# Layer norm, attention and a gated branch on one core: hi/lo splits of later chunks moved to POOL from a plain copy, and PSUM banks released by tile

## The chip, the cores and the metric

The kernel runs on one core of a Trainium2 chip. The metric is device time in microseconds (us), the median of several runs. TensorE (PE in the profile, PEld its weight loads) multiplies into PSUM; VectorE (DVE), ScalarE (ACT) and GpSimd (POOL) work beside it; SyncE (SP) issues the DMAs of this kernel, in its own order. In this kernel POOL works on SBUF tiles only, never on PSUM.

## The reference

```
xn = layernorm(x)                                     # x: 2048 x 512, eps 1e-5
q, k, v = split(xn @ wqkv)                            # 32 heads of 16
p = softmax(q @ k.T / 4)                              # per head
s = (p @ v, heads joined) @ wo
g = silu(((xn @ w_gate) * (xn @ w_up)) @ w_down)      # w_gate, w_up: 512 x 1792
out = x + s * g
```

All of it is float32. The kernel reaches its precision on a reduced matmul type by splitting each operand into a high half (rounded) and a low half (the rest), and adding three products: high x high, high x low, low x high. So a matrix that is to be multiplied needs two halves, and making them is the work that this case is about.

## The kernel before, in words

The 2048 rows are 16 tiles of 128 (`tt`), in four chunks of 512 (`c`). The kernel has three stages.

**The prologue** is `early()` (L614 to L709). It loads the rows and weights, norms and turns chunk 0, and then issues 265 numbered steps. Each step takes the next matmul of a stream that goes through k(0), q(0), v of tiles 0 to 2, k(1), q(1), v 3, k(2), v 4 and 5, k(3), v 6 to 15 (L694): k(c) and q(c) are the projections of chunk c for the first group of heads, 12 matmuls each. A table (`at`, L678 to L693) hangs other work on steps: the statistics of a tile (`ln_stats`, L170), the root (`ln_root`, `ve`, L178), the scale (`ln_scale`, L181, a chain of six small VectorE operations, L184 to L189, the first a reciprocal), the normalization (`ln_apply`, on ScalarE but for one tile), and the turning (`ln_turn`, L198). Turning transposes a tile with four matmuls into one PSUM bank; then ScalarE reads the bank and writes the high half `xh` (L204), and VectorE reads the bank again and writes the low half `xl` (L211). A projection ends likewise: ScalarE writes the high half `hl[:, 0]` (`qk_high`, L277), VectorE the low half from the same bank (`qk_out`, L281), and SP stores both to DRAM and reloads them in the layout that the scores want (`qk_store`, `load_k`, `load_q`).

The list `EARLY` (L39) puts groups of four score matmuls on the steps 57, 66, 75, 84 (keys of chunk 0), 98, 108, 118, 128 (chunk 1), 138 and on (chunk 2), 178 and on (chunk 3). A score bank is free when VectorE has reduced it to its maxima (`mx`, L549).

The prologue's PSUM pool (`EARLY_BUFS`, L40) has four banks for scores and the first four turned tiles ("s"), two for the other turned tiles and q(0) ("x"), and two for projections ("f"). Then `banks_of` (L88) opens another pool (`BUFS`, L41) on the same eight banks: two for the transposed scores "st", three "s", one "pv", two "misc".

**The middle** (L778 to L808) has 512 rounds: four transposed-score matmuls (`t`, L572), their exponentials on ScalarE (L574), four score matmuls of a later group (`s`, L547), the sums over values (`pv`, L583), and some matmuls of a filler: the other projections (`proj_pair`, where POOL already makes the halves from an SBUF copy `qr`, L271 and L272), and the gated branch.

**The tail** is the last filler (`ending`, L424): the output projection in pairs of tiles into the two "misc" banks (`z`, L238 and L242), and for each tile `end` (L408): a product with the gate, a sum with x, and a store. In the last 21 rounds and behind them VectorE does both (L411, L412): the product goes back into the PSUM bank, and the sum reads it there. Up to then VectorE does the product (L414) and POOL the sum (L415).

Within PE, ACT and DVE the order of instructions is the order in which the program writes them (`manual_schedule` with `ORDERED`, L44). For SP and POOL a scheduler chooses the order when the program is built. In all cases an engine works its instructions off in its order, so a waiting one holds those behind it.

Of the kernel before, what the change touches and what calls it, by code (L numbers as in the profile page):

```python
# [11 lines left out]
F32 = mybir.dt.float32  # L12
# [34 lines left out]
def body(ctx, tc, x, wqkv, wo, wg, wu, wd, out):  # L47
# [4 lines left out]
    def dma(dst, src):  # L52
        nc.sync.dma_start(dst, src)
# [33 lines left out]

    def banks_of(bufs):  # L88
        stack = ExitStack()
        fst["ps"] = stack.enter_context(tc.tile_pool(name="ps" + "".join(bufs), bufs=1, space=PSUM)), bufs  # L90
        return stack

    def psum(tag, name):
# [47 lines left out]
        nc.gpsimd.tensor_tensor(lo, raw, hi, op=OP.subtract)  # L141
        return hi, lo

    def split_rows(src, raw, wh, wl, queue, early):
        for d in range(len(raw)):
            queue.dma_start(raw[d], src[d * P:(d + 1) * P])
            if early:
                nc.scalar.activation(wh[d], raw[d], AF.Copy)
            else:
                nc.gpsimd.tensor_copy(wh[d], raw[d])  # L150
            nc.gpsimd.tensor_tensor(wl[d], raw[d], wh[d], op=OP.subtract)
        return wh, wl

    norm = {}

    def tokens(tt):
# [38 lines left out]
            return nc.vector.tensor_scalar(xt, xt, e[:, t:t + 1], mr[:, t:t + 1], op0=OP.mult, op1=OP.add)  # L195
        return nc.scalar.activation(xt, xt, AF.Identity, bias=mr[:, t:t + 1], scale=e[:, t:t + 1])

    def ln_turn(tt, low=True):  # L198
        c, t = divmod(tt, 4)
        xt = tokens(tt)  # L200
        norm["x", tt] = pt = psum("x" if c else "s", f"xT{tt}")
        for d in range(ND):
            nc.tensor.transpose(pt[:, d * P:(d + 1) * P], xt[:, d * P:(d + 1) * P], ident)
        nc.scalar.activation(xh[c][:, :, t * P:(t + 1) * P], pt.rearrange("p (d q) -> p d q", d=ND), AF.Copy)  # L204
        if low:
            ln_low(tt)

    def ln_low(tt):
        c, t = divmod(tt, 4)
        sl = slice(t * P, (t + 1) * P)  # L210
        nc.vector.tensor_tensor(xl[c][:, :, sl], norm["x", tt].rearrange("p (d q) -> p d q", d=ND), xh[c][:, :, sl],  # L211
                                op=OP.subtract)
# [40 lines left out]
    def qk_proj(w, m, which, c, tag):  # L253
        wh, wl = w
        o = psum(tag, f"p{which}_{m}_{c}")
        hi, lo = [lambda d, w=w: w[:, d] for w in (wh, wl)]
        yield from full(o, ((hi, lambda d: xh[c][:, d]), (lo, lambda d: xh[c][:, d]), (hi, lambda d: xl[c][:, d])))
        qk_out(o, qk_high(o), m, which, c)

    def proj_pair(m, which):  # L260

        outs = []
        yield from pair(outs, [("misc", f"p{w}_{m}_{c}") for _, w, c in which],
                        [terms(lambda d: ws[0][:, d], lambda d: ws[1][:, d],
                               lambda d: xh[c][:, d], lambda d: xl[c][:, d], ND) for ws, _, c in which])
        raws = [qp.tile([P, D], F32, name="qr", bufs=2) for _ in outs]
        fst["high"] = nc.scalar.activation(raws[0], outs[0], AF.Copy)
        nc.vector.tensor_copy(raws[1], outs[1])
        for o, (_, w, c) in zip(raws, which):
            hl = qp.tile([P, 2, D], F32R, name="hl", bufs=HBUFS)  # L270
            nc.gpsimd.tensor_copy(hl[:, 0], o)  # L271
            nc.gpsimd.tensor_tensor(hl[:, 1], o, hl[:, 0], op=OP.subtract)  # L272
            qk_store(hl, m, w, c)

    def qk_high(o):
        hl = qp.tile([P, 2, D], F32R, name="hl", bufs=HBUFS)
        nc.scalar.activation(hl[:, 0], o, AF.Copy)  # L277
        return hl

    def qk_out(o, hl, m, which, c):  # L280
        nc.vector.tensor_tensor(hl[:, 1], o, hl[:, 0], op=OP.subtract)  # L281
        qk_store(hl, m, which, c)

    def qk_store(hl, m, which, c):

# [36 lines left out]
    def ffn(nxt):  # L322
        fp = fst["fp"]
        for c in range(NC):
# [7 lines left out]
            for ti, fs in enumerate(THIRDS):  # L332
# [20 lines left out]
                if c == NC - 1 and fs[-1] == NF - 1:  # L353
                    fst["y"] = y
                    fst["w"] = [keep.tile([P, ND, D], F32R, name=n) for n in ("fh", "fl")]
                    for d in range(ND):
                        raw = fp.tile([P, D], F32, name="wdr", bufs=2)
                        split_rows(wo[d * P:(d + 1) * P], [raw], *[[t[:, d]] for t in fst["w"]], nc.sync, False)
                for t in range(0, 4, 2):
                    outs = []  # L360
                    yield from pair(outs, [("misc", f"y{c}_{ti}_{u}") for u in (t, t + 1)], [terms(lambda i: hh[:, i, u * P:(u + 1) * P],
# [45 lines left out]

    def end(c, t, o, yt, xt):  # L408
        tt = 4 * c + t
        if now[0] >= NU * 16 - LEAD and c < NC - 1 or t % 2 and c == NC - 1:  # L410
            nc.vector.tensor_tensor(o, o, yt, op=OP.mult)  # L411
            nc.vector.tensor_tensor(yt, o, xt, op=OP.add)  # L412
        else:
            nc.vector.tensor_tensor(yt, o, yt, op=OP.mult)  # L414
            nc.gpsimd.tensor_tensor(yt, yt, xt, op=OP.add)  # L415
        dma(out[tt * P:(tt + 1) * P], yt)

    def o_terms(c, t):
# [195 lines left out]
    def early():  # L614
# [17 lines left out]
        def warm(n):  # L632
            for _ in range(n):
                nc.tensor.matmul(psum("x", "warm"), ident, on.rearrange("p b e -> p (b e)"), start=True, stop=True)
# [11 lines left out]
            ln_apply(tt)  # L646
        ln_stats(3)
        ln_root(first[1])
        ln_turn(0, False)
        ln_turn(1, False)  # L650
        warm(1)
        ln_scale(first[1])
        last = ln_apply(2)
        ln_apply(3)
# [1 line left out]
        ln_low(1)  # L656
        ln_turn(2)
        ln_turn(3)
        warm(1)
        wk, wq = [split_raw(f"w{which}", raw, last) for which, raw in zip((1, 0), wraw)]  # L660
        wv = [[etile().bitcast(F32R) for _ in range(ND)] for _ in range(2)]
        for d in range(ND):
# [172 lines left out]
```

## Time and profile before

| what | value |
|---|---|
| median of 3 runs | 1809.49 us (1808.87 to 1809.57) |
| the profiled execution's own time | 1810.38 us |
| its span | 1808.6 us |
| PE busy | 1791.0 us, 99% |
| DVE busy | 1480.3 us, 82% |
| ACT busy | 1237.7 us, 68% |
| POOL busy | 548.3 us, 30% |
| granted TensorE clock, mean | 0.999 of full |

The span is the time between the first and last instruction of the profiled execution; its own time has 1.8 us around that. PE's matmuls overlap, so a row with several matmuls that is longer than the same row elsewhere holds a wait that isn't shown as idle. Where a row says `[1.29 <-DVE xl L211]`, the engine stood idle for 1.29 us before it, until that instruction let it go.

### The profile page before, as it was taken

How to read it: one execution, taken by the hardware profiler on the slowest of the kernel's cores; microseconds unless marked ns; L12 is line 12 of the kernel's file. 1: busy time of each engine (PE TensorE's matmuls, PEld its weight loads, DVE VectorE, ACT ScalarE, POOL GpSimd, SP SyncE). 2: the span in 40 equal slices, each digit the busy share in tenths (PEclk: the TensorE clock that was granted, in tenths of full speed). 3: DMA queues.
4: the chain of work that ended last, by engine and by line, in shares of the span. 5: the costliest groups of instructions: out<-in, count | busy, mean ns of one | idle time of the engine just before them, and what ended most of it. 6: DMA issues, size and time to landing. Idle time of an engine off the chain costs nothing.

```text
span 1808.6 us, 34173 instructions
## 1 busy us (share of the span) xinstructions
PE 1791.0 (99%) x13572; PEld 991.8 (55%) x13572; DVE 1480.3 (82%) x2472; ACT 1237.7 (68%) x2365; POOL 548.3 (30%) x615
## 2 busy tenths in 40 slices
PE   8999999999999999999999999999999999999998
PEld 5655555555555555555555555555555555555555
DVE  7878888888888888888888888888888888888832
ACT  5257676777776767777677777776767767767664
POOL 2012322531322234233132441431325323224340
PEclk9999999999999999999999999999999999999999
DMA  5515422611231132311124220511125111111342
GB/s 199 142 63 201 177 106 112 161 46 33 63 74 49 37 99 75 74 51 51 28 65 110 68 63 24 103 51 40 43 80 120 48 44 51 40 42 51 116 154 71
DMA packets 117228, 145.73 MB, mean 81 GB/s; under 512 B 12620, under 2 KB 74060, under 8 KB 114380
## 3 DMA queue, kind: packets, MB, share of 16 engines
q1 hardware_dynamic: 117068, 143.55, 27.8%
q8 instruction: 106, 1.74, 0.4%
q14 instruction: 54, 0.44, 0.1%
HBM read 95.94 MB, written 47.45 MB: 79 GB/s over the span
## 4 chain that ended last, share of the span: by engine, by line
PE 95%; DVE 2%; DMA 1%; ACT 1%; issue 0%; POOL 0%; SPq 0%; DVEq 0%; ACTq 0%
PE pv L583 28%; PE t L572 21%; PE s L547 12%; PE y L238 6%; PE u L238 5%; PE g L238 5%; PE u L242 4%; PE g L242 4%; PE p L238 3%; PE y L242 2%; PE v L219 2%; PE z L238 1%; PE z L242 1%; PE p L242 1%; DMA ks<-KD 0%
## 5 line engine op out<-in xcount | busy, mean ns | idle before, releaser
L549 DVE TENSOR_REDUCE mx<-s 128x1 f32<-128x512 f32 x2048 | 1312.0, 684 | 246.1 <-PE s L547 156.0
L574 ACT ACTIVATE e<-t 128x512 f32<-128x512 f32 x2048 | 1111.7, 596 | 430.5 <-PE s L547 267.3
L572 PE MATMUL t<-qs,ks 50*128 50x512 f32 x2048 | 705.1, 426 | 1.6 <-ACT V L299 0.8
L547 PE MATMUL s<-ks,qs 48*128 48x512 f32 x2048 | 699.9, 427 | 0.8 <-DMA ks<-KD 0.6
L572 PEld LDWEIGHTS t<-qs,ks 50*128 50x128 f32 x2048 | 347.2, 185 | 500.8 <-ACT e L574 473.1
L583 PE MATMUL pv<-e,V 128*32 128x512 f32 x4096 | 545.7, 605 | 0.0
L547 PEld LDWEIGHTS s<-ks,qs 48*128 48x128 f32 x2048 | 337.6, 184 | 23.5 <-DVE mx L549 7.3
L583 PEld LDWEIGHTS pv<-e,V 128*32 128x32 f32 x4096 | 81.0, 108 | 156.4 <-issue 147.2
L138 POOL CAST w0h<-w0r 128x512 fp32r<-128x512 f32 x60 | 36.7, 611 | 414.9 <-PE u L238 216.0
L351 POOL CAST dh<-wdr 128x512 fp32r<-128x512 f32 x56 | 33.6, 611 | 184.0 <-PE y L242 103.1
L242 PE MATMUL u<-fh,w0h 64*128 64x512 f32 x224 | 88.2, 394 | 0.4 <-DVE h L347 0.4
L242 PE MATMUL y<-dh,hh 64*128 64x512 f32 x224 | 88.2, 394 | 0.0
L238 PE MATMUL u<-fh,w0l 64*128 64x512 f32 x224 | 87.8, 392 | 0.0
L238 PE MATMUL g<-fh,w1l 64*128 64x512 f32 x224 | 87.8, 392 | 0.0
L238 PE MATMUL u<-fh,w0h 64*128 64x512 f32 x224 | 87.6, 391 | 0.0
L238 PE MATMUL g<-fl,w1h 64*128 64x512 f32 x224 | 87.6, 391 | 0.0
L238 PE MATMUL y<-dh,hl 64*128 64x512 f32 x224 | 87.6, 391 | 0.0
L242 PE MATMUL g<-fl,w1h 64*128 64x512 f32 x224 | 87.6, 391 | 0.0
L238 PE MATMUL u<-fl,w0h 64*128 64x512 f32 x224 | 87.6, 391 | 0.0
L238 PE MATMUL y<-dh,hh 64*128 64x512 f32 x224 | 87.5, 391 | 0.0
L238 PE MATMUL g<-fh,w1h 64*128 64x512 f32 x224 | 87.5, 391 | 0.0
L238 PE MATMUL y<-dl,hh 64*128 64x512 f32 x224 | 87.5, 391 | 0.0
(249 smaller groups left out, 2853.0 us busy)
## 6 DMA issues: line engine op xcount, KB each, us to landing
w1r<-in_wg_dram SPq DMA_DIRECT2D x56, 256.0 KB
w0r<-in_wu_dram SPq DMA_DIRECT2D x56, 256.0 KB
wdr<-in_wd_dram SPq DMA_DIRECT2D x56, 256.0 KB
qs<-QD SPq DMA_DIRECT2D x64, 192.0 KB
ks<-KD SPq DMA_DIRECT2D x12, 768.0 KB
KD<-hl SPq DMA_DIRECT2D x16, 512.0 KB
QD<-hl SPq DMA_DIRECT2D x16, 512.0 KB
OD<-tr SPq DMA_DIRECT2D x31, 256.0 KB
```

The lines of the kernel that those rows point to most:

```text
L138: cast = nc.gpsimd.tensor_copy(hi, raw)
L219: nc.tensor.matmul(o, l(d), r(d), start=k == d == 0, stop=k == 2 and d == ND - 1)
L238: nc.tensor.matmul(outs[k], l[LOWER], r[LOWER], start=k == 0 and n == 0, stop=(stop or k == 0) and n == len(low) - 1, skip_group_check=k == 1)
L242: nc.tensor.matmul(outs[1 - k], l[UPPER], r[UPPER], start=k == 0 and m == 0, stop=(stop or k == 0) and m == len(high) - 1, skip_group_chec ...
L351: nc.gpsimd.tensor_copy(dh[:, i], raw)
L547: nc.tensor.matmul(o, QS[i][b:b + KB, pr, t * P:(t + 1) * P], k[b:b + KB, pr, kc * 512:(kc + 1) * 512], start=True, stop=True)
L549: nc.vector.tensor_reduce(MX[i][:, j, t, kc:kc + 1], o, axis=AX.X, op=OP.max)
L572: nc.tensor.matmul(o, k[b:b + KR, pr, kt * P:(kt + 1) * P], QS[i][b:b + KR, pr], start=True, stop=True)
L574: nc.scalar.activation(e, o, AF.Exp, scale=DH ** -0.5)
L583: nc.tensor.matmul(fst["pv"][32 * j:32 * j + 32], V[:, kt, h0:h0 + 32], es[j], start=kt == 0, stop=kt == NT - 1)
```

## The change

For chunks 1 to 3, `ln_turn` and `qk_proj` call a new function `halves`: ScalarE makes a plain float32 copy of the PSUM bank into an SBUF tile `qr`, and POOL makes the high half and the low half from that copy. `qr` has three buffers instead of two. Chunk 0 keeps ScalarE and VectorE. The two single `warm` matmuls between the first turned tiles go. `banks_of` opens its pools with `reuse_waits="tile"`: a tile that lies on a bank of a closed pool waits for the tiles that lay on that bank, and not for the whole pool. In `end`, a late tile writes the product to SBUF, where the sum then reads it. `proj_pair` and the split of `wo` call the new `split_rows` and issue what they issued before.

```diff
@@ -87,7 +87,7 @@
 
     def banks_of(bufs):
         stack = ExitStack()
-        fst["ps"] = stack.enter_context(tc.tile_pool(name="ps" + "".join(bufs), bufs=1, space=PSUM)), bufs
+        fst["ps"] = stack.enter_context(tc.tile_pool(name="ps" + "".join(bufs), bufs=1, space=PSUM, reuse_waits="tile")), bufs
         return stack
 
     def psum(tag, name):
@@ -140,16 +140,6 @@
             tc.add_manual_dep(cast.ins, after.ins.name, BEHIND, reason="keeps the port free for the layer norm")
         nc.gpsimd.tensor_tensor(lo, raw, hi, op=OP.subtract)
         return hi, lo
-
-    def split_rows(src, raw, wh, wl, queue, early):
-        for d in range(len(raw)):
-            queue.dma_start(raw[d], src[d * P:(d + 1) * P])
-            if early:
-                nc.scalar.activation(wh[d], raw[d], AF.Copy)
-            else:
-                nc.gpsimd.tensor_copy(wh[d], raw[d])
-            nc.gpsimd.tensor_tensor(wl[d], raw[d], wh[d], op=OP.subtract)
-        return wh, wl
 
     norm = {}
 
@@ -195,15 +185,30 @@
             return nc.vector.tensor_scalar(xt, xt, e[:, t:t + 1], mr[:, t:t + 1], op0=OP.mult, op1=OP.add)
         return nc.scalar.activation(xt, xt, AF.Identity, bias=mr[:, t:t + 1], scale=e[:, t:t + 1])
 
-    def ln_turn(tt, low=True):
+    def halves(o, hi, lo):
+
+        raw = qp.tile([P, D], F32, name="qr", bufs=3)
+        first = nc.scalar.activation(raw, o, AF.Copy)
+        split_rows(raw, hi, lo)
+        return first
+
+    def split_rows(raw, hi, lo):
+        if len(hi.shape) == 3:
+            raw = raw.rearrange("p (d q) -> p d q", d=ND)
+        nc.gpsimd.tensor_copy(hi, raw)
+        nc.gpsimd.tensor_tensor(lo, raw, hi, op=OP.subtract)
+
+    def ln_turn(tt):
         c, t = divmod(tt, 4)
         xt = tokens(tt)
         norm["x", tt] = pt = psum("x" if c else "s", f"xT{tt}")
         for d in range(ND):
             nc.tensor.transpose(pt[:, d * P:(d + 1) * P], xt[:, d * P:(d + 1) * P], ident)
-        nc.scalar.activation(xh[c][:, :, t * P:(t + 1) * P], pt.rearrange("p (d q) -> p d q", d=ND), AF.Copy)
-        if low:
-            ln_low(tt)
+        hi, lo = [x[c][:, :, t * P:(t + 1) * P] for x in (xh, xl)]
+        if c:
+            halves(pt, hi, lo)
+        else:
+            nc.scalar.activation(hi, pt.rearrange("p (d q) -> p d q", d=ND), AF.Copy)
 
     def ln_low(tt):
         c, t = divmod(tt, 4)
@@ -255,7 +260,13 @@
         o = psum(tag, f"p{which}_{m}_{c}")
         hi, lo = [lambda d, w=w: w[:, d] for w in (wh, wl)]
         yield from full(o, ((hi, lambda d: xh[c][:, d]), (lo, lambda d: xh[c][:, d]), (hi, lambda d: xl[c][:, d])))
-        qk_out(o, qk_high(o), m, which, c)
+        hl = qp.tile([P, 2, D], F32R, name="hl", bufs=HBUFS)
+        if c:
+            halves(o, hl[:, 0], hl[:, 1])
+        else:
+            nc.scalar.activation(hl[:, 0], o, AF.Copy)
+            nc.vector.tensor_tensor(hl[:, 1], o, hl[:, 0], op=OP.subtract)
+        qk_store(hl, m, which, c)
 
     def proj_pair(m, which):
 
@@ -263,23 +274,13 @@
         yield from pair(outs, [("misc", f"p{w}_{m}_{c}") for _, w, c in which],
                         [terms(lambda d: ws[0][:, d], lambda d: ws[1][:, d],
                                lambda d: xh[c][:, d], lambda d: xl[c][:, d], ND) for ws, _, c in which])
-        raws = [qp.tile([P, D], F32, name="qr", bufs=2) for _ in outs]
+        raws = [qp.tile([P, D], F32, name="qr", bufs=3) for _ in outs]
         fst["high"] = nc.scalar.activation(raws[0], outs[0], AF.Copy)
         nc.vector.tensor_copy(raws[1], outs[1])
         for o, (_, w, c) in zip(raws, which):
             hl = qp.tile([P, 2, D], F32R, name="hl", bufs=HBUFS)
-            nc.gpsimd.tensor_copy(hl[:, 0], o)
-            nc.gpsimd.tensor_tensor(hl[:, 1], o, hl[:, 0], op=OP.subtract)
+            split_rows(o, hl[:, 0], hl[:, 1])
             qk_store(hl, m, w, c)
-
-    def qk_high(o):
-        hl = qp.tile([P, 2, D], F32R, name="hl", bufs=HBUFS)
-        nc.scalar.activation(hl[:, 0], o, AF.Copy)
-        return hl
-
-    def qk_out(o, hl, m, which, c):
-        nc.vector.tensor_tensor(hl[:, 1], o, hl[:, 0], op=OP.subtract)
-        qk_store(hl, m, which, c)
 
     def qk_store(hl, m, which, c):
 
@@ -355,7 +356,8 @@
                     fst["w"] = [keep.tile([P, ND, D], F32R, name=n) for n in ("fh", "fl")]
                     for d in range(ND):
                         raw = fp.tile([P, D], F32, name="wdr", bufs=2)
-                        split_rows(wo[d * P:(d + 1) * P], [raw], *[[t[:, d]] for t in fst["w"]], nc.sync, False)
+                        dma(raw, wo[d * P:(d + 1) * P])
+                        split_rows(raw, *[t[:, d] for t in fst["w"]])
                 for t in range(0, 4, 2):
                     outs = []
                     yield from pair(outs, [("misc", f"y{c}_{ti}_{u}") for u in (t, t + 1)], [terms(lambda i: hh[:, i, u * P:(u + 1) * P],
@@ -407,12 +409,13 @@
 
     def end(c, t, o, yt, xt):
         tt = 4 * c + t
-        if now[0] >= NU * 16 - LEAD and c < NC - 1 or t % 2 and c == NC - 1:
+        if t % 2 and c == NC - 1:
             nc.vector.tensor_tensor(o, o, yt, op=OP.mult)
             nc.vector.tensor_tensor(yt, o, xt, op=OP.add)
         else:
+            late = now[0] >= NU * 16 - LEAD and c < NC - 1
             nc.vector.tensor_tensor(yt, o, yt, op=OP.mult)
-            nc.gpsimd.tensor_tensor(yt, yt, xt, op=OP.add)
+            (nc.vector if late else nc.gpsimd).tensor_tensor(yt, yt, xt, op=OP.add)
         dma(out[tt * P:(tt + 1) * P], yt)
 
     def o_terms(c, t):
@@ -646,9 +649,8 @@
             ln_apply(tt)
         ln_stats(3)
         ln_root(first[1])
-        ln_turn(0, False)
-        ln_turn(1, False)
-        warm(1)
+        ln_turn(0)
+        ln_turn(1)
         ln_scale(first[1])
         last = ln_apply(2)
         ln_apply(3)
@@ -656,7 +658,8 @@
         ln_low(1)
         ln_turn(2)
         ln_turn(3)
-        warm(1)
+        ln_low(2)
+        ln_low(3)
         wk, wq = [split_raw(f"w{which}", raw, last) for which, raw in zip((1, 0), wraw)]
         wv = [[etile().bitcast(F32R) for _ in range(ND)] for _ in range(2)]
         for d in range(ND):
```

## Rows read from the trace of the kernel before

**Rows 1.** The page, part 4: the chain that ended last, by engine.

```profile
PE 95%; DVE 2%; DMA 1%; ACT 1%; issue 0%; POOL 0%; SPq 0%; DVEq 0%; ACTq 0%
```

**Rows 2.** Waits; PE's timeline; a window (last three: PEclk, DMA share, GB/s).

```profile
PE xT L203 <- DVE xl L211: 2.4, 3, 1.3
...
13.77 1.17 PE L219 MATMUL p<-fh,w1h 128*128 128x512 f32 x4
...
33.77 1.90 PE L547 MATMUL s<-ks,qs 48*128 48x512 f32 x4
...
43.61 0.66 PE L203 MATMUL xT<-ident,V 128*128 128x128 f32 x4 [1.29 <-DVE xl L211]
...
48.61 0.73 PE L219 MATMUL p<-xh,w1h 128*128 128x512 f32 x2 [0.69 <-ACT V L299]
...
50.53 0.71 PE L547 MATMUL s<-ks,qs 48*128 48x512 f32 x3 [0.32 <-DMA ks<-KD]
...
12.00:14.00 2.00, 2.00 (x11) 1.23 (x11) 1.82 (x4) 1.52 (x4) 2.00 (x3) 1.00 1.05 396
```

**Rows 3.** Timeline of ACT, 10 to 66 us.

```profile
12.54 1.08 ACT L204 ACTIVATE fh<-xT 128x512 fp32r<-128x512 f32 x2 [0.48 <-PE xT L203]
...
24.71 0.58 ACT L204 ACTIVATE xh<-xT 128x512 fp32r<-128x512 f32 x1
...
55.18 0.59 ACT L277 ACTIVATE hl<-p 128x512 fp32r<-128x512 f32 x1
```

**Rows 4.** Timeline of DVE, 10 to 66 us.

```profile
18.15 1.17 DVE L178 TENSOR_SCALAR ve<-mv 128x4 f32<-128x4 f32 x1
...
19.81 0.76 DVE L185 TENSOR_TENSOR e<-r 128x4 f32<-128x4 f32 x1
...
24.28 0.67 DVE L173 BATCH_NORM_STATS2 st<-V 128x6 f32<-128x512 f32 x1
...
27.37 0.16 DVE L189 SCALAR_TENSOR_TENSOR mr<-mv,e 128x4 f32<-128x4 f32 x1
...
32.64 2.48 DVE L549 TENSOR_REDUCE mx<-s 128x1 f32<-128x512 f32 x4
```

**Rows 5.** POOL's timeline; then groups by line and form (busy, mean ns, idle before).

```profile
15.49 5.06 POOL L664 TENSOR_TENSOR e<-e 128x512 fp32r<-128x512 f32 x4
...
L272 POOL TENSOR_TENSOR hl<-qr,hl 128x512 fp32r<-128x512 f32 x26 | 33.0, 1289 | 0.0
...
L271 POOL CAST hl<-qr 128x512 fp32r<-128x512 f32 x26 | 15.2, 612 | 73.6 <-ACT qr L267 73.6
...
L211 DVE TENSOR_TENSOR xl<-xT,xh 128x512 fp32r<-128x512 f32 x12 | 8.1, 682 | 4.7 <-ACT xh L204 4.7
```

**Rows 6.** Timeline of SP, the DMA issues, 0 to 130 us.

```profile
39.22 0.83 SPq L56 DMA_DIRECT2D KD<-hl  x2
45.41 0.32 SPq L56 DMA_DIRECT2D QD<-hl  x1
...
46.41 0.93 SPq L56 DMA_DIRECT2D ks<-KD  x2
```

**Rows 7.** Timelines of PE and ACT, 64 to 126 us.

```profile
65.78 0.70 PE L547 MATMUL s<-ks,qs 48*128 48x512 f32 x3 [0.30 <-DMA ks<-KD]
...
106.96 0.46 PE L572 MATMUL t<-qs,ks 50*128 50x512 f32 x1 [0.79 <-ACT V L299]
...
106.27 0.60 ACT L299 ACTIVATE V<-v 128x512 f32<-128x512 f32 x1 [3.05 <-PE v L219]
```

**Rows 8.** Groups by line and form; one line's instructions (ns); POOL's timeline.

```profile
L242 PE MATMUL z<-fh,hl 64*128 64x512 f32 x32 | 12.8, 401 | 2.4 <-DVE hh L412 1.7 <-DVE dl L412 0.8
...
L412 DVE TENSOR_TENSOR dl<-z,dl 128x512 f32<-128x512 f32 x6 | 4.1, 692 | 0.2
...
L505 DVE TENSOR_TENSOR h<-tr,g x1: 693/693/693, 1796.8 to 1796.8; 128x512 fp32r<-128x512 f32 x1
...
1738.88 1.27 POOL L313 TENSOR_TENSOR y<-e,y 128x512 f32<-128x512 f32 x1
```

## The prediction, made before the change was run

> **What bounds the kernel now.** I read the page first: TensorE holds 95% of the chain that ended last [rows 1]. The middle, rounds of scores, exponentials and filler matmuls, has TensorE work back to back, and the change leaves its instructions alone; what moves lies in the prologue (0 to 107 us), at its end, and in the closing pairs of the output projection (from about 1724 us). There I read the timeline of TensorE for its gaps, and then the timelines of the engines named as releasers. Work on PE is in order, so a wait that goes there moves everything behind it, unless the next thing is late instead.
>
> In the prologue PE waits three times, 2.4 us in all, for the VectorE subtraction `xl` that still reads the PSUM bank which the next transposition wants; the longest is 1.29 us at 43.61 [rows 2]. A hidden one is the score group at step 66: four matmuls spread over 1.90 us from 33.77, since VectorE is late with the maxima of the group before [rows 2, 4]. Then 0.69 us at 48.61 before k(2), shown as a wait for a `V` copy; but its bank is that of q(1), which VectorE (L281) lets go at the same moment. Then 0.32 us at 50.53 for the keys of chunk 1 [rows 2] and 0.30 us at 65.78 for those of chunk 2 [rows 7].
>
> **The change, part by part. (a) Turned tiles.** For chunks 1 to 3 ScalarE makes a plain copy and POOL the two halves. ScalarE's instruction stays one PSUM read of about 0.6 us [rows 3]; VectorE loses 12 subtractions of about 0.68 us and four more in the projections; POOL gains 16 pairs, a cast of 0.61 and a subtraction of 1.29 us [rows 5], 1.9 us each, 30 us in all. POOL had nothing to do there from 20.55 us on [rows 5]. A bank is now free after ScalarE (25.29 for tile 4 [rows 3]), about 0.7 us sooner, so the three waits of 2.4 us go.
>
> What is late next: VectorE's layer-norm chain. At 18.15 `ve` took 1.17 us and at 19.81 the first multiply 0.76 us, where such operations otherwise take about 0.16 [rows 4]. Four POOL subtractions ran end to end from 15.49 to 20.55 [rows 5], 1.26 us apart, so the third ended near 19.3; the two held operations ended at 19.32 and 20.57. So a small VectorE operation of this kind waits for the end of the running POOL instruction; the reciprocal and the statistics between them were not held. The changed kernel puts POOL to work on tiles 4 to 7 from 25.3 to 32.8, right where chunk 2's chain runs. Its `ve` still comes ahead, at 25.1, behind the last statistics of 24.28 [rows 4]. Then L185 to L189, five operations, each reach the port while POOL is busy: ends at about 26.0, 27.2, 27.8, 28.4 to 29.0, and 29.7, against 27.53 before [rows 4]. Behind it on VectorE stand four statistics (0.67 us and a short second step each [rows 4], 3.3 us in all), without the two subtractions that used to lie among them; then the maxima of step 57 start at 33.05 against 32.64 [rows 4]. The step-66 scores need those banks, so PE leaves them 0.3 us **later** than before: the first two bank waits (1.1 us) are not collected. Bounds: 1.4 us gained here if nothing is held, 1.0 us lost if the maxima slip by one POOL subtraction more. I take the loss of 0.3, since the two held rows are this very chain.
>
> The Trainium skill ("GPSIMD Engine Reference", Performance versus the Vector engine) has the Vector engine about 2 times faster on elementwise work, which speaks against moving it. The rows agree on the price, 1.29 against about 0.69 us; by that rule alone the prologue would lose, but here the moved work has an idle engine, and what counts is only when each result is needed.
>
> From there: 1.29 us at 43.61 goes (chunk 3's chain, at 35.5 to 36.7, lies in a POOL gap, and the copy of tile 9 ends near 41.3, ahead of PE at 42.7). **(b) Projections.** q(1)'s bank is free after ScalarE's copy, by my reckoning near 44.4, so 0.69 us goes; k(2) could start at 46.95. It needs POOL's cast of tile 11. POOL's queue there is k(1), tiles 8 to 11, then q(1), 1.9 us each from 38.3: tile 11's cast ends by 46.7, q(1) at 49.9. It just fits.
>
> The keys of chunk 1: k(1)'s halves end at 40.2 (before, VectorE gave them at 39.2 and SP issued at once [rows 6]). A store and its reload need about 7 us (keys of chunk 2: halves done 59.0, used at 65.78 [rows 7]); 47.1 us is ahead of the need at 48.3, so the 0.32 us goes too. For chunk 2 POOL is still behind: q(1) to 49.9, tiles 12 to 14, then k(2), copied by ScalarE near 53.3 (55.18 before [rows 3]); its halves end at 57.4, the scores can start 6.8 us later, 64.2, and PE is there at 63.8: a wait of 0.4 more. Against 65.78 [rows 7] that is 1.6 us gained: +0.3 - 1.29 - 0.69 - 0.32 + 0.4. Chunk 3's keys have 0.9 us to spare.
>
> **(c) Two warm matmuls** leave PE's queue. The second pair ends where the first projection starts, 13.77, and that needs ScalarE's cast of tile 3, done at 13.62 [rows 2, 3]: 0 to 0.1 us gained. Moving `ln_low(2)` and `ln_low(3)` behind the transpositions leaves VectorE's order as it is: nothing.
>
> **(d) Banks by tile.** PE stands 0.79 us at 106.96 until the last `V` copy (106.27 to 106.87) is done, though the score-transposed matmul it wants to start writes another bank [rows 7]. Released by tile, that one can start at about 106.2; the pair of projections behind it probably takes the banks of that copy and of the last maxima, so it comes at about 106.95 instead of 107.49. I take 0.5, with 0 and 0.79 as ends.
>
> **(e) The end of late tiles.** The product now leaves PSUM at once, and the sum has both operands in SBUF; it is not faster (0.693 us for such an operation, 0.692 for the old form [rows 8]), but the second bank of a pair is free before its sum, not after. PE waits there 2.4 us, 1.7 in two places and 0.8 in a third [rows 8]. Freed 0.69 us earlier each, unless POOL holds the first sum: at 1777 POOL is idle (0.69), at 1738 its short operation ends just before (0.55; the subtraction of 1.27 us starts behind it [rows 8]), at 1724 it is in a run (0.36). Sum 1.6. Ends: 2.1 with no hold; with a hold through a whole subtraction at two places, 0.8 us lost at each, so a loss of 0.9. The final tiles on the chain of the last transposition have as many operations as before: nothing.
>
> For the sum in (e), the Trainium skill ("Advanced Engine Details and Errata", VectorE Performance Modes; the GPSIMD page adds the case of two SBUF inputs) has POOL and such VectorE instructions block each other. The two held rows of the layer norm agree; by that rule each sum waits, without it the 2.1 stands.
>
> **Sum.** 1.6 + 0.05 + 0.5 + 1.6 = 3.75 us. The profiled execution took 1810.38 us around a span of 1808.6, 0.89 above the median of 1809.49; so 1806.6 for it, and 1805.7 for the median.
>
> **The rivals.** *Keys behind the queries (slower).* SP is one queue. In the kernel before it issued the keys' load (46.41) only behind the first query store (45.41), though the key store had gone at 39.22 [rows 6]. If that order stays, the load waits for POOL's cast of q(1), the last in its queue, at 48.6, so it goes at 49.7, 3.3 us later, and the scores come 3.3 us after 50.53. With 0.5 and 1.6 regained, that is 1.2 us slower: 1810.7. It decides where the cast of q(1) comes later than about 43 us and the order is kept. Against it: the store has 8 us until then, not 6, so an order by readiness puts the load first. 10%.
>
> *Nothing is held.* If VectorE's chain slips between POOL's instructions, step 66 gains 1.4 instead of losing 0.3; some is lost again to the keys of chunk 2. 1.4 us more: 1804.3. Against it stand the two held rows. 13%.
>
> *The edges give nothing.* The sums in the tail are held and the banks at the prologue's end still wait: only 1.6 of the prologue remains, 1807.9. 12%.
>
> *The clock falls.* Without the warm pairs TensorE idles a little more before 13.77. The granted clock stood at full there [rows 2]; at the lower level (1.2 GHz) the twelve k(0) matmuls, in fours of 1.17 us at most [rows 2], about 2.8 us in all, would take twice that: about 1808.5. The transpositions lie between, so 5%.
>
> **The numbers.** The forecast holds 60%, with its own range 1804.7 to 1807.2. About 0.2% (3.6 us) is what a measurement of this kernel can tell from no change, and 1805.9 is that line: a little over half of the forecast and nearly all of the second rival lie below it. More than 0.2% slower takes the first rival with a held tail (1813), or a cost that I don't see: 9%. The range 1803.8 to 1809.7 takes in all but the first rival and small tails.
>
> **What would show it.** Right: no gap of PE behind `xl`, L185 to L189 of chunk 2 stretched to 4 us, the maxima of step 57 near 33, scores of chunk 2 near 64, first exponential near 106.9, and gaps before the z pairs down to about 0.1 to 0.4 us. Wrong: a gap of PE over 2 us for `ks<-KD`, the chain at 1.5 us beside a busy POOL, or sums in the tail over 1 us.

## The result, and the profile after

The changed kernel takes 1817.24 us (median of 6 runs, 1816.54 to 1819.25), the kernel before, run beside it, 1809.53 (1808.87 to 1810.88): 7.7 us slower, ratio 1.0044 (95% interval 1.0031 to 1.0057). The forecast was 1805.7, with 1803.8 to 1809.7 as its range. The span of the profiled execution grew from 1808.6 to 1815.7 us.

The page's part 4, the chain that ended last, by engine (it answers to [rows 1]), and of part 2 the granted clock in 40 slices:

```profile
PE 94%; DVE 2%; DMA 2%; POOL 1%; issue 0%; ACT 0%; SPq 0%; POOLq 0%; ACTq 0%; DVEq 0%
...
PEclk9899999999999999999999999999999999999999
```

The share of DMA went from 1 to 2%, and the second slice, 45 to 91 us, has a clock under 9 tenths. So the loss lies in the prologue. There TensorE's waits, from 10 to 125 us (engine, line, releaser; total, times, longest), read:

```profile
PE s L550 <- DMA ks<-KD: 8.8, 4, 7.0
...
PE p L224 <- ACT fh L211: 0.8, 1, 0.8
```

The three waits for `xl` of [rows 2], 2.4 us, are gone as the change means them to. In their place stand 8.8 us for the keys, which took 0.6 us before. (The second line is the stretch ahead of k(0) where a warming matmul used to run; k(0) starts no later for it.) TensorE's timeline shows where; these rows answer to [rows 2, 7]:

```profile
13.18 1.17 PE L224 MATMUL p<-fh,w1h 128*128 128x512 f32 x4 [0.83 <-ACT fh L211]
...
33.20 2.29 PE L550 MATMUL s<-ks,qs 48*128 48x512 f32 x4 [0.32 <-DVE mx L552]
...
46.23 0.74 PE L224 MATMUL p<-xh,w1h 128*128 128x512 f32 x2
...
54.39 0.76 PE L550 MATMUL s<-ks,qs 48*128 48x512 f32 x1 [6.98 <-DMA ks<-KD]
55.42 1.19 PE L550 MATMUL s<-ks,qs 48*128 48x512 f32 x3 [0.26 <-DMA ks<-KD]
...
61.82 0.42 PE L206 MATMUL xT<-ident,V 128*128 128x128 f32 x2
...
73.69 0.46 PE L550 MATMUL s<-ks,qs 48*128 48x512 f32 x1 [1.24 <-DMA ks<-KD]
74.47 0.70 PE L550 MATMUL s<-ks,qs 48*128 48x512 f32 x3 [0.32 <-DMA ks<-KD]
...
116.34 0.50 PE L575 MATMUL t<-qs,ks 50*128 50x512 f32 x1
```

Up to 46.23, where k(2) starts, TensorE is 2.38 us ahead of the 48.61 of [rows 2] (0.59 of it because the first rows were ready sooner: k(0) starts at 13.18 against 13.77). Then, within one step, it is 4.9 us behind: the scores of step 98 stand at 55.42 against 50.53 [rows 2]. Why the keys are late is in SyncE's timeline (issue time and duration), which answers to [rows 6]:

```profile
39.88 0.83 SPq L56 DMA_DIRECT2D KD<-hl  x2
49.21 0.80 SPq L56 DMA_DIRECT2D QD<-hl  x2
50.11 1.41 SPq L56 DMA_DIRECT2D ks<-KD  x2
```

The keys were stored at 39.88. Their load has its place in the queue behind **both** stores of q(1), where in [rows 6] it stood behind one. One of the two carries the low half of q(1), and POOL gives that last, as its timeline shows:

```profile
45.55 0.62 POOL L198 CAST xh<-qr 128x512 fp32r<-128x512 f32 x1
46.11 0.63 POOL L198 CAST hl<-qr 128x512 fp32r<-128x512 f32 x1
46.68 1.28 POOL L199 TENSOR_TENSOR xl<-qr,xh 128x512 fp32r<-128x512 f32 x1
47.91 1.28 POOL L199 TENSOR_TENSOR hl<-qr,hl 128x512 fp32r<-128x512 f32 x1
```

The subtraction ends at 49.19 and the first of the two stores goes at 49.21. The load also took longer to land. From its issue to the last three scores it is 5.3 us (50.11 to 55.42), where it was 4.1 before (46.41 to 50.53 [rows 2, 6]). The likely reason is that the store of both halves (512 KB, the other 256) now goes ahead of it and not behind: the windows below show the 16 DMA engines 0.99 and 0.95 busy while it moved. No run separates this. So of the 4.9 us by which step 98 is late, 3.7 are the later issue (50.11 against 46.41) and 1.2 the landing.

A second price hangs on the first. Windows of 2 us (busy time of PE, PEld, DVE, ACT and POOL; then PEclk, DMA share, GB/s):

```profile
50.00:52.00 2.00, 0.00 (x0) 0.00 (x0) 0.00 (x0) 0.00 (x0) 1.08 (x1) 0.91 0.99 367
52.00:54.00 2.00, 0.00 (x0) 0.00 (x0) 0.00 (x0) 0.00 (x0) 0.00 (x0) 0.50 0.95 224
...
56.00:58.00 2.00, 2.00 (x7) 1.07 (x5) 1.78 (x3) 0.00 (x0) 0.00 (x0) 0.50 0.09 9
...
62.00:64.00 2.00, 2.00 (x14) 1.28 (x13) 1.07 (x2) 1.09 (x2) 0.85 (x3) 1.00 0.03 8
```

In the wait the granted clock fell to the lower level (0.50 is 1.2 of 2.4 GHz), and it stayed there to nearly 62 us: 7 matmul records in a full window where later there are 14. From the last scores of step 98 to the turn of tile 14 TensorE needed 6.40 us (55.42 to 61.82). The kernel before needed 3.52: its turn of tile 14 came at 54.05. That is 2.9 us more.

At the keys of chunk 2 there is a wait again, 1.24 and 0.32 us, and behind it the clock reads 0.50 from 76 to 78. From 116 us on the distance hardly changes: 9.4 us at the first transposed scores (116.34 against 106.96 [rows 7]), 9.2 at the first product of the late tiles (near 1733), and 7.1 at the end, since the new end of late tiles gives 2 us back.

### The profile page after: what moved, and what is told of

It reads as the page before. It is cut to its first block, busy times and chain, and to the rows that moved or that the text cites. A ratio compares the mean times of both kernels' runs of the same rounds, so it can differ in the third digit from the quotient of the medians.

```text
span 1815.7 us, 34194 instructions
## 1 busy us (share of the span) xinstructions
PE 1794.1 (99%) x13568; PEld 991.1 (55%) x13568; DVE 1474.4 (81%) x2456; ACT 1238.3 (68%) x2365; POOL 580.7 (32%) x647
## 4 chain that ended last, share of the span: by engine, by line
PE 94%; DVE 2%; DMA 2%; POOL 1%; issue 0%; ACT 0%; SPq 0%; POOLq 0%; ACTq 0%; DVEq 0%
PE pv L586 27%; PE t L575 21%; PE s L550 11%; PE y L243 6%; PE u L243 5%; PE g L243 4%; PE u L247 4%; PE g L247 4%; PE y L247 3%; PE p L243 3%; PE v L224 2%; PE p L247 2%; PE z L243 1%; PE z L247 1%; DMA wdr<-in_wd_dram 1%; PE p L224 0%
## 5 line engine op out<-in xcount | busy, mean ns | idle before, releaser
L247 PE MATMUL g<-fh,w1h 64*128 64x512 f32 x224 | 87.7, 392 | 0.0
L243 PE MATMUL g<-fh,w1h 64*128 64x512 f32 x224 | 87.7, 391 | 0.0
```

What stands on the lines that cost most here:

```text
L243: nc.tensor.matmul(outs[k], l[LOWER], r[LOWER], start=k == 0 and n == 0, stop=(stop or k == 0) and n == len(low) - 1, skip_group_check=k == 1)
L247: nc.tensor.matmul(outs[1 - k], l[UPPER], r[UPPER], start=k == 0 and m == 0, stop=(stop or k == 0) and m == len(high) - 1, skip_group_chec ...
```

## The experiments

All runs are the median of this kernel against the kernel before on the same chip in the same rounds; the befores lay between 1809.33 and 1810.11.

**Keys first.** The changed kernel; a dependency puts the two stores of q(1) behind the load of chunk 1's keys in SyncE's queue.

```diff
...
-        dmar(dst[:, both], hl)
-        dmar(dst[:, one], hl[:, 0])
+        puts = dmar(dst[:, both], hl), dmar(dst[:, one], hl[:, 0])
+        if m == 0 and which == 0 and c == 1:
+            for put in puts:
+                tc.add_manual_dep(put.ins, fst["keys"].ins.name, ORDER, reason="keys of chunk 1 go first")
...
```

> The changed kernel, with one edge of order more on SP: q(1)'s two stores stand behind the load of chunk 1's keys. Theory A (the order on SP, and the clock that falls in the wait, are the whole loss): the keys' load is issued near 43 us, step 98 waits under 0.5 us, the granted clock stays at full from 44 to 84 us, and the time is 1804 to 1807. Rival B (POOL delivers the halves of k(1) too late, whatever the order): most of the 7 us wait stays, over 1812. Rival C (another edit, such as the warm matmuls or the held layer norm, costs the rest): the wait goes, but the time stays over 1809.5.

Measured: 1806.38 us (1803.43 to 1808.5), ratio 0.9980 (0.9972 to 0.9989). SyncE's timeline, and what waits are left on TensorE's:

```profile
40.84 0.83 SPq L57 DMA_DIRECT2D KD<-hl  x2
...
44.21 0.80 SPq L57 DMA_DIRECT2D ks<-KD  x2
...
50.20 0.81 SPq L57 DMA_DIRECT2D QD<-hl  x2
```

```profile
64.25 0.47 PE L553 MATMUL s<-ks,qs 48*128 48x512 f32 x1 [1.44 <-DMA ks<-KD]
65.09 0.70 PE L553 MATMUL s<-ks,qs 48*128 48x512 f32 x3 [0.38 <-DMA ks<-KD]
```

With nothing but the order mended the change is 3.25 us faster than before instead of 7.71 slower; the order is worth 11 us. The load went 3.4 us after its store, and step 98 no longer waits. Two things that theory A expected did not come: keys of chunk 2 are still late by 1.8 us, and behind that wait the clock reads 0.50 from 68 to 70 us.

**The split alone.** The changed kernel with the old `end` and the old release of banks; the splits on POOL stay, the warming matmuls stay out.

```diff
...
-        if t % 2 and c == NC - 1:
+        if now[0] >= NU * 16 - LEAD and c < NC - 1 or t % 2 and c == NC - 1:
...
-            (nc.vector if late else nc.gpsimd).tensor_tensor(yt, yt, xt, op=OP.add)
+            nc.gpsimd.tensor_tensor(yt, yt, xt, op=OP.add)
```

> The changed kernel with the old end of tiles and the old release of PSUM pools; the splits on POOL and the missing warm matmuls stay. Theory A: SP's order is the changed kernel's, so the wait of about 7 us and the low clock stay, and the gains at the prologue's end and in the tail (0.6 and 2.0 us by the two traces) are gone: 1819 to 1820.5. Rival C (a part of the loss comes from the new end or the new release): under 1817.

Measured: 1818.15 us (5 runs), ratio 1.0046 (1.0034 to 1.0059), with a wait of 6.50 us at step 98. That is 0.9 us under the range of the theory and 1.2 above the rival's line; all of the loss is in this part. **The end alone** and **the banks alone**, each on the kernel before:

```diff
-        if now[0] >= NU * 16 - LEAD and c < NC - 1 or t % 2 and c == NC - 1:
+        if t % 2 and c == NC - 1:
...
+            late = now[0] >= NU * 16 - LEAD and c < NC - 1
...
-            nc.gpsimd.tensor_tensor(yt, yt, xt, op=OP.add)
+            (nc.vector if late else nc.gpsimd).tensor_tensor(yt, yt, xt, op=OP.add)
```

> The kernel before with the new end of late tiles alone. Theory A: the three waits before z shrink from 2.4 to about 0.7 us, as in the changed kernel, 1807 to 1808. Rival (sums held by POOL give it back): 1809.3 to 1810.

> The kernel before with PSUM banks released by tile alone. Theory A: the 0.79 us gap at the prologue's end goes in part, 1808.7 to 1809.1. Rival (the pair behind it waits for the same banks): 1809.4 to 1809.6.

Measured: the end 1807.71 us, ratio 0.9988 (0.9979 to 0.9997), 1.9 us faster; the banks 1808.91, ratio 0.9995 (0.9986 to 1.0004), 0.7 us, which the interval does not tell from nothing. In the trace of the banks' run the 0.79 us before the first transposed scores [rows 7] is gone (this run's k(0) began at 12.83, 0.94 sooner than in [rows 2], so not all of the 2 us between 104.91 and 106.96 is the banks'):

```profile
104.91 0.50 PE L572 MATMUL t<-qs,ks 50*128 50x512 f32 x1
```

**The wait filled.** The changed kernel with eight matmuls of a constant tile in the wait.

```diff
         at[190].append((ones_rows, ks[0]))
+        at[98].append((warm, 8))
```

> The changed kernel with eight matmuls of the constant tile put into step 98, ahead of the scores that wait for the keys of chunk 1. Their results are read by nobody. The wait itself (6.98 us in the changed kernel) stays: the load of the keys still goes behind both stores of q(1). Only what TensorE does in it is different. Theory (the wait costs twice, once by itself and once by the lower granted clock behind it): the granted clock stays near 1.00 from 52 to 62 us, steps 98 to 101 take about 3.5 us as before and not 6.4, and the time falls by about 2.9 us from 1817.2 to about 1814.3, or to about 1812.8 if the second dip at 76 to 78 us, which came after a wait of 1.8 us, goes as well. Rival (the low clock is not bound to the idle stretch but to what TensorE runs then): the clock falls as before and the time stays at 1817 or goes above it.

Measured: 1812.55 us (11 runs, 1811.43 to 1813.76), ratio 1.0013 (1.0004 to 1.0021). TensorE's timeline, and two windows:

```profile
48.49 7.21 PE L637 MATMUL warm<-on,ident 128*128 128x512 f32 x16
55.63 1.24 PE L550 MATMUL s<-ks,qs 48*128 48x512 f32 x4
```

```profile
52.00:54.00 2.00, 2.00 (x6) 0.94 (x5) 0.00 (x0) 0.00 (x0) 0.00 (x0) 1.00 1.05 307
...
56.00:58.00 2.00, 1.95 (x12) 1.33 (x11) 1.84 (x4) 0.00 (x0) 0.00 (x0) 1.00 0.49 86
```

The keys come as late as in the changed kernel, but the clock stays at full behind them. Against its own before the kernel is 2.4 us slower instead of 7.7: **5.3 of the 11 us hang on TensorE standing idle in that wait**, and the rest, from 2.4 slower to the 3.25 gained with the order mended, 5.7 us, is the wait itself. The two traces show where the 5.3 us lie. The first dip is 2.9 of them. At chunk 2 the wait is 0.8 us shorter (0.37 and 0.36 instead of 1.24 and 0.32), and the dip behind it is gone: from its last three scores to the next group takes 3.1 us (71.44 to 74.58), where the changed kernel took 4.7 (74.47 to 79.18). So some 4.5 us are the lower clock. The rival falls.

**The order alone.** The kernel before, its splits untouched; only the load is put behind both stores.

```diff
...
+                    if g == 0 and cs == [1]:
+                        for put in fst["puts"]:
+                            tc.add_manual_dep(load.ins, put.ins.name, ORDER, reason="queries of chunk 1 go first")
...
```

> The kernel before, with its splits where they were, where only the load of the keys of chunk 1 is put behind both stores of q(1) in SyncE's queue (it stood behind one of them). Theory (it is the order in the queue that makes the loss, and the POOL splits make it long): the low half of q(1) is ready on VectorE about 2 us earlier than on POOL, so the load goes at about 47 to 48.5 us instead of 46.41, the scores of step 98 wait 0.5 to 2.5 us and the clock may dip; 1810 to 1814 us. Rival (the order does not matter while VectorE splits q(1)): the load still lands ahead of TensorE's need and the time stays within 0.2% of before, 1808 to 1811 us.

Measured: 1815.87 us (6 runs, 1815.51 to 1817.62), ratio 1.0032 (1.0020 to 1.0043), more than either theory gave. SyncE's timeline and TensorE's:

```profile
47.84 0.33 SPq L57 DMA_DIRECT2D QD<-hl  x1
48.28 1.19 SPq L57 DMA_DIRECT2D ks<-KD  x2
```

```profile
52.35 0.76 PE L550 MATMUL s<-ks,qs 48*128 48x512 f32 x1 [3.37 <-DMA ks<-KD]
53.39 1.19 PE L550 MATMUL s<-ks,qs 48*128 48x512 f32 x3 [0.28 <-DMA ks<-KD]
```

The load goes 1.9 us later than the 46.41 of [rows 6], or 2.7 counted from k(0), which began 0.8 sooner here (12.97). It lands late as well, 5.1 us from its issue to the last three scores (48.28 to 53.39), as in the changed kernel. That brings waits of 3.4 and 0.3 us, a clock of 0.50 from 52 to 56, and 5.8 us in all. So the order loses time even where VectorE makes the split.

**The queries split the old way**, with the keys first; and the same **with the two warming matmuls** put back.

```diff
...
-        if c:
+        if c and which:
             halves(o, hl[:, 0], hl[:, 1])
...
```

> The changed kernel with the keys of chunk 1 loaded ahead of the stores of q(1), and with the projection q(1) split the old way, high half by ScalarE and low half by VectorE; the keys' projections and the turned tiles stay with POOL. Theory (what is left of the waits, 1.4 and 0.4 us at the keys of chunk 2, comes from q(1)'s two POOL instructions standing ahead of the tiles and of k(2) in POOL's queue): these waits go or fall under 0.5 us, and the time falls by 1 to 2.5 us from 1806.4 to 1804 to 1805.4. Rival (POOL catches up between the chunks, and the wait at chunk 2 comes from the order of SyncE's queue): the waits stay and the time stays at 1806.4 give or take 0.7.

> The kernel of the run before this one with the two warming matmuls of the prologue, which the change took out, put back in their places. Theory (they cost what they last where TensorE was the last to be ready, and the clock does not need them): 0 to 1 us slower than without them. Rival (they keep the granted clock up in the first 16 us or at 36 to 40 us, where dips showed in single profiles): as fast or up to 1 us faster, with fewer slices under 1.00 in the first 70 us.

Measured: 1806.62 us (ratio 0.9981, 0.9972 to 0.9989), and 1806.09 with the warming matmuls (ratio 0.9982, 0.9973 to 0.9991). My theory of the wait at chunk 2 missed: it stayed, 1.6 and 1.9 us. The warming matmuls cost nothing that these runs can tell. POOL's timeline of the second run shows what delays the keys instead:

```profile
51.90 0.62 POOL L199 CAST hl<-qr 128x512 fp32r<-128x512 f32 x1
52.48 1.30 POOL L200 TENSOR_TENSOR xl<-qr,xh 128x512 fp32r<-128x512 f32 x1
53.73 1.28 POOL L200 TENSOR_TENSOR hl<-qr,hl 128x512 fp32r<-128x512 f32 x1
```

Between the two halves of k(2) stands a tile's subtraction, 1.3 us, and the half itself takes twice VectorE's time. So the next runs took the keys off POOL as well.

**Only the tiles on POOL.** The changed kernel, with all projections split as before; no order set by hand.

```diff
-        if c:
-            halves(o, hl[:, 0], hl[:, 1])
-        else:
-            nc.scalar.activation(hl[:, 0], o, AF.Copy)
-            nc.vector.tensor_tensor(hl[:, 1], o, hl[:, 0], op=OP.subtract)
+        nc.scalar.activation(hl[:, 0], o, AF.Copy)
+        nc.vector.tensor_tensor(hl[:, 1], o, hl[:, 0], op=OP.subtract)
```

> The changed kernel with the turned tiles of chunks 1 to 3 split by POOL, as the change has it, but with every projection of later chunks (k(1), q(1), k(2), k(3)) split as before, high half by ScalarE and low half by VectorE; no order is set by hand. In SyncE's queue the load of the keys of chunk 1 then stands behind one of the two stores of q(1), as in the kernel before. Theory (the loss comes from the projections' part of the change alone, by the place that the load gets): no wait over 1 us for keys at step 98, and 1803.5 to 1806.5 us, with the gain of the end, the banks and most of the prologue. Rival (the tiles' part makes POOL or VectorE late too, so that VectorE holds the low half of q(1) back): the load goes after 49 us and the time stays above 1811.

Measured: 1804.59 us (6 runs, 1803.9 to 1805.73), ratio 0.9971 (0.9960 to 0.9983). SyncE's timeline has the old order again, and TensorE's has waits of 0.6 us at most for keys:

```profile
42.62 0.32 SPq L56 DMA_DIRECT2D QD<-hl  x1
...
43.62 0.93 SPq L56 DMA_DIRECT2D ks<-KD  x2
44.97 0.34 SPq L56 DMA_DIRECT2D QD<-hl  x1
```

```profile
46.87 0.49 PE L547 MATMUL s<-ks,qs 48*128 48x512 f32 x1 [0.64 <-DMA ks<-KD]
...
62.76 0.69 PE L547 MATMUL s<-ks,qs 48*128 48x512 f32 x3 [0.47 <-DMA ks<-KD]
```

Which engines split the four projections k(1), q(1), k(2) and k(3) is the whole difference to the changed kernel, and it is worth 12.5 us (7.71 + 4.74).

**All mended**: the same with the keys first and the warming matmuls in.

> The same split as in the run before this one, with the keys of chunk 1 loaded ahead of both stores of q(1) and the two warming matmuls put back. Theory (with k(2) no longer behind a tile's subtraction in POOL's queue its store goes about 2 us sooner, so the wait of 1.9 us at the keys of chunk 2 goes, and with it the dip of the clock behind it): 1802 to 1804.5 us. Rival (the wait at chunk 2 is set by store and load, some 6.5 us from the one to the landing of the other, whatever splits k(2)): a wait over 1 us stays at step 138 and the time stays at 1806.1 give or take 0.7.

Measured: 1803.24 us (5 runs, 1803.19 to 1805.4), ratio 0.9966 (0.9953 to 0.9978). Against the run with the warming matmuls only the keys' splits differ, and its wait of 1.9 us is down to 0.6; the dip behind it is gone.

```profile
64.28 0.70 PE L550 MATMUL s<-ks,qs 48*128 48x512 f32 x3 [0.58 <-DMA ks<-KD]
```

**Later steps** and **the second wait filled** leave the keys on POOL (both start from the run with the warming matmuls).

```diff
...
-EARLY = [57, 66, 75, 84] + [98 + 10 * n for n in range(17)]
+EARLY = [57, 66, 75, 84] + [98 + 10 * n + max(0, min(8, 12 - n)) * (n > 3) for n in range(17)]
```

```diff
...
+        at[138].append((warm, 2))
```

> The kernel with keys first, q(1) split the old way and the warming matmuls (1806.09 us), where the scores of chunk 2 and those after them come later in the order written out by hand: steps 146, 155, 164, up to 209, instead of 138, 148, up to 208, so that eight matmuls of projections stand in the place of the wait. Theory (wait and dip together cost 1.9 and about 1.7 us, and other work can stand there): no key wait over 0.5 us, granted clock 1.00 from 60 to 70 us, and 1802.5 to 1804.5 us. Rival (the projections and the maxima that come closer together wait in their turn): 1806 give or take 0.7.

> The kernel with keys first, q(1) split the old way and the warming matmuls (1806.09 us), with two matmuls of the constant tile at step 138, in the wait for the keys of chunk 2; their results are read by nobody. The wait for the keys stays and only TensorE's idleness goes. Theory (the dip behind the short wait costs about 1.7 us and comes from the idle stretch): granted clock 1.00 from 60 to 70 us and 1804 to 1805 us. Rival (the dips behind short waits come and go without them): a dip stays there, or the time stays at 1806.1 give or take 0.5.

Measured: later steps 1803.58 us (5 runs, 1801.31 to 1804.7), ratio 0.9962 (0.9949 to 0.9974); no wait is left on TensorE from 40 to 80 us and the clock is at full from 40 on. The filled wait 1805.72 us (11 runs, ratio 0.9981, 0.9972 to 0.9990): its profile has the clock at full, as the theory said, but the time is the rival's. The clock was not at full in all of its runs: their mean granted clocks go from 1.000 (1804.66 to 1806.58 us) down to 0.998 (1807.96 and 1808.12). So what the second dip costs is not settled by this pair (by the traces it is 1.6 us in the changed kernel, as above); that real work in the wait's place gains some 2 us is.

So the two best versions are only the tiles on POOL with the keys first (1803.24), and the keys on POOL with the scores of chunk 2 up to eight steps later (1803.58). Their intervals overlap with each other, and with that of only the tiles on POOL with no order set (1804.59).

## Why the prediction was wrong

- **(a) and the first half of (b): right.** It took the first two bank waits as uncollected, with the step-66 scores 0.3 us later than before. They end at 35.49, against 35.67 for the row of [rows 2]; less the 0.59 us by which all began sooner, that is 0.4 later. The reason held too. VectorE's timeline, which answers to [rows 4], beside POOL's:

```profile
25.46 1.31 DVE L176 TENSOR_TENSOR e<-e,ve 128x4 f32<-128x4 f32 x1
26.81 0.53 DVE L177 TENSOR_SCALAR e<-e 128x4 f32<-128x4 f32 x1
...
27.57 1.14 DVE L179 SCALAR_TENSOR_TENSOR mr<-mv,e 128x4 f32<-128x4 f32 x1
...
31.95 0.61 DVE L168 TENSOR_SCALAR ve<-mv 128x4 f32<-128x4 f32 x1
32.47 1.87 DVE L552 TENSOR_REDUCE mx<-s 128x1 f32<-128x512 f32 x3
```

```profile
25.46 1.30 POOL L199 TENSOR_TENSOR xl<-qr,xh 128x512 fp32r<-128x512 f32 x1
...
27.40 1.29 POOL L199 TENSOR_TENSOR xl<-qr,xh 128x512 fp32r<-128x512 f32 x1
```

  Two operations of the chain end with POOL's subtractions, at 26.8 and 28.7, and the one between with POOL's cast. With the 0.59 put back the chain ends at 29.3, where I had 29.7, and the maxima begin at 33.06, where I had 33.05. That they agree so well is luck: the next `ve` was held too, for 0.61 us instead of 0.16, which I did not have. Nor is the chain held alike in each execution. In the profile of the run with the warming matmuls the maxima begin 1.4 us sooner, counted from k(0), and the step-66 scores take 1.31 us instead of 2.29. The terms -1.29 and -0.69 came in: k(2) starts 1.8 us sooner beyond the 0.59, where the sum had 1.7.
- **The step that failed** is the sentence in (b) on the keys of chunk 1: "47.1 us is ahead of the need at 48.3". It counted from the halves (40.2) to the use as if the load went when its store had landed. The load went at 50.11, in its place behind the stores of q(1), and was used at 54.39. So the term was not -0.32 but a loss of 7 us, and it brought a term that the sum did not have, the lower clock behind the wait. At the keys of chunk 2 the wait was 1.6 us where the sum had 0.4, with a dip of its own.
- **The first rival had the mechanism and not the price.** "Keys behind the queries" named the queue, the place and the row that gave it away. It gave 1810.7, out by 6.5 us, for three reasons. It let the load wait for the cast of q(1) alone, as one store did in [rows 6], and not for the subtraction. That its 49.7 came near the 50.11 is luck, since the cast was done at 46.7 and not at 48.6. It let the load land as fast as before, so the scores were to come 3.3 us later, where they came 4.9 later. And it priced no clock, which is the largest part. The argument against it, that the store has 8 us until then, was a guess about the scheduler: what makes it choose was not tried. Runs show only that the order comes with the projections' split on POOL and goes without it.
- **The clock rival looked in the wrong place**, ahead of 13.77. The clock fell where TensorE stood for 7 us, and with what followed at chunk 2 that cost 5.3 us. What the Trainium skill says ("TensorE: Matmul & The Clock Gate", Part 1), that the lower level is the default and activity is what lifts it, agrees: the row at 52 to 54 us has no matmul and 0.50, and with matmuls in that stretch it reads 1.00.
- **(c)** held as far as it can be told: with and without the two matmuls 1806.09 and 1806.62.
- **(d)** 0.5 forecast, 0.7 measured, within what the interval leaves open.
- **(e)** 1.6 forecast, 1.9 measured alone. The waits ahead of the z pairs fell from 2.4 to 0.8 us (the group answers to [rows 8]); the sums were held in three pairs, for 0.87 to 1.07 us instead of 0.69, none of them through a whole POOL subtraction:

```profile
L247 PE MATMUL z<-fh,hl 64*128 64x512 f32 x32 | 12.8, 400 | 0.8 <-DVE hh L417 0.4 <-DVE dl L417 0.3
```

With the order mended, the measurement (3.25 us) comes near the sum (3.75), in part by luck. The end and the banks alone gave 1.9 and 0.7, by medians, so some 0.6 is left for a prologue that was to give 1.6: the keys of chunk 2 were 1.8 us late instead of 0.4, with a dip behind them. Where neither was seen, with only the tiles on POOL, the gain is 4.74. The terms (a), (d) and (e) were near what was measured; the order of SyncE's queue and the clock were not in the sum.

## What to carry to other kernels

When a store's data comes later, look at what stands behind that store in its DMA queue: a load that has been ready for some 7 us waits with it (stored at 39.88, and 3.4 us from store to load where nothing stood between), and the program order does not show it where a scheduler orders the queue. Price a wait of several microseconds on TensorE twice, once as time and once as the lower clock behind it, or put useful work in its place. Of the work that an idle slow engine could take, give it what is needed late (here the tiles), and keep on the fast engines what feeds a store and a reload (here keys and queries).

## What the runs showed of the hardware that was not expected

- Large instructions of VectorE and POOL stretch each other. The tail of the changed kernel, VectorE's timeline and POOL's:

```profile
1748.61 1.06 DVE L418 TENSOR_TENSOR hh<-hh 128x512 f32<-128x512 f32 x1
```

```profile
1747.51 1.61 POOL L314 TENSOR_TENSOR y<-e,y 128x512 f32<-128x512 f32 x1
```

  The sum took 1.06 us instead of 0.69 and POOL's product 1.61 instead of 1.27 [rows 8]. The small ones of the layer norm were held to POOL's end and did not stretch it (1.30 us).
- Short waits can be followed by the lower clock too. In the run with the keys first a wait of 1.44 and 0.38 us stands before a clock of 0.50 from 68 to 70 us; with waits of 0.6 us and less at that place none was seen. But shorter ones are no safeguard. The run with the end alone has the prologue of the kernel before, and behind its waits of 0.69 us ahead of k(2) and 0.34 us for the keys of chunk 1 the clock fell, where the profile of the kernel before has 1.00 behind waits of 0.69 and 0.32:

```profile
50.00:52.00 2.00, 2.00 (x7) 1.60 (x7) 2.00 (x4) 0.00 (x0) 0.00 (x0) 0.53 0.33 90
52.00:54.00 2.00, 2.00 (x9) 1.62 (x7) 1.06 (x2) 0.60 (x1) 0.00 (x0) 0.62 0.57 113
```

- Six of the 14 profiles have a dip at 36 to 40 us (0.51 from 36 to 38 in the run with the keys first). In all six the step-66 scores ahead of it take 2.3 us, stretched by waits for VectorE's maxima, of which the row shows 0.3 as idle. The changed kernel and the run with the second wait filled have the same stretch and no dip; the six profiles whose scores take 0.94 to 1.97 us have none. From these scores to the turn of tile 8 the run with the queries split the old way took 5.72 us with the dip (33.23 to 38.95) and the changed kernel 4.20 without it (33.20 to 37.40), so the dip costs 1.5 us there. The run with the warming matmuls took 3.21 (33.12 to 36.33), with neither the dip nor the stretch.
- That runs of one kernel lie up to 5 us apart goes in part with the clock. Each run has a mean granted clock: with the queries split the old way the quickest (1803.79) is the only one at 1.000 and the other ten have 0.997 to 0.999; with the later steps 1801.31 and 1801.69 have 1.000, 1804.38 and 1804.7 have 0.998. It is not the whole: with all mended the run at 1.000 took 1804.0 and one at 0.998 took 1803.21. Why the clock falls in one execution and not in the next stays open.
